# Some 25 entries of a fused four-layer kernel's order tables moved by one step or less

## The chip, the cores and the metric

The kernel runs on one core of one Trainium2 chip. The metric is device time in microseconds (us) of one launch; the figure for a kernel is the median of its runs. All engines of the core are in use: TensorE for matmuls (PE, and PEld for its weight loads), VectorE (DVE), ScalarE (ACT), GpSimd (POOL), and SyncE (SP), which here does nothing but issue DMAs.

## The reference

Four residual layers A, B, A, B on x of 2048 tokens by 512, fp32, 32 heads of 16. Layer A is linear attention with a learned feature map (per head a 16x16 product, then softmax of it and of its negative). Layer B cuts the sequence into four segments of 512 tokens; in each it does causal softmax attention and mixes it with a read of a memory that the segments before it have filled.

```python
# layer A
pq, pk = einsum(q, w_phi), einsum(k, w_phi)
phi = lambda t: concatenate([softmax(t), softmax(-t)])
kv, z = einsum("bhsf,bhsd->bhfd", phi(pk), v), phi(pk).sum over s
o = (phi(pq) @ kv) / (phi(pq) . z + 1e-6);  x = x + o @ wo
# layer B, for each of the four segments s
p = softmax(qs @ ks.T * scale + causal mask);  a_dot = p @ vs
a_mem = (elu1(qs) @ M) / (elu1(qs) . z + 1e-6)
o = g * a_mem + (1 - g) * a_dot
M, z = M + elu1(ks).T @ vs, z + elu1(ks).sum();  x = x + o @ wo
# both layers take layernorm(x) as input
```

## The kernel before

Matrix products of weight and activation are done as three products of a high and a low part (`hh`/`hl`, `oh`/`ol`, the two `w` tiles). The program is one long list: every engine takes its instructions in the order in which the Python code emits them (`Ordered` and `held` add a dependency from each instruction to the one before it on its engine). What is emitted when is set by tables of text. So an instruction that waits holds up everything behind it on its own engine.

Layer A has two passes. Pass 2 of a layer A runs into the layer B that follows: `A20` of its pieces are emitted before B's steps begin, and the rest is given out in the slots from step -9 to step 1 until `LEFT` units of TensorE work are spent.

Layer B is a loop over steps `k` from `BEGIN` = -25 to 163. One layer B has 32 pairs of head groups `m` (8 per segment), and each takes five steps, so a segment has 40 steps. A cell `5.1` of segment 2 is step 2 x 40 + 5 x 5 + 1 = 106. Cells of segment 0 stand in `FIRST`, of segments 1 and 2 in `GAPS`, of segment 3 in `LAST` (first layer B) or `FINAL` (second one), steps below 0 in `BEFORE`. In each step there is a fixed part, in this order:

1. `attend`: two to four products into the PSUM tile `lg`, of which there is one buffer; ACT takes exp of it in one instruction of 128x1024 (`P<-lg`), POOL masks diagonals. The next step's `lg` can't begin before this exp has ended.
2. `maxima`: products into the PSUM tiles `mx` and `my`, one buffer each, and DVE reductions of them (`junk` or `mx`/`my` out, `mxs` the result). The next step's `mx` product waits for these reductions.
3. `weighted` in some steps: the products `pv<-P,v`, 16 of them in a row.

Around that stand the table's entries, and things that are due at a half step after another event (`at`, `due`). The entries and events that the change and the prediction speak of:

- `out/2`: two quarters of an output projection of the segment before (three products `g<-w,oh`, `g<-w,oh`, `g<-w,ol` to a quarter); the last quarter ends with a DVE add `xr<-g,xr`. `x2` loads that `xr` row.
- `q2+/1`, `v/2`, `p/3`: quarters of a projection of the next segment, of the next layer's values, of the last output projection.
- `ln`: four transposes of a normalized tile of the next layer's input (`g<-ident,x`), an ACT copy (`hh<-g`) and a DVE subtraction (`hl<-g,hh`).
- `t1` (transposes of keys, copied by ACT), `m2` (update of the memory), `a3` (read of the memory: `pv<-tb,mem`, `g<-tb,mem`, then ACT copies `ot<-pv` and `mmq<-g`), `fin` (`g<-ident,U`, DVE division), `pt` (`end_turn`: transposes, `ot<-g,ot`, `oh<-ot`, `ol<-ot,oh`).
- `max` (`put_maxima`): a transpose `g<-ident,mxs`, an ACT copy `mt<-g`, and a DMA.
- `JOIN`: when a finished output block is scaled and added (POOL), copied to its high part by ACT (`oh<-tmp`, fourth number) and reduced to its low part by POOL (`ol<-tmp,oh`, fifth). Its three rows hold for segment 0, segments 1 and 2, and segment 3.
- `INVERT`: denominators gathered by a DMA (`dm<-den` or `dn<-den`), inverted by DVE (`RECIPROCAL`), stored and loaded again. `READ[2]` shifts this whole chain for the two blocks of segment 3 that get only their memory part so.
- `GATHER`: when the two DMAs from a finished `U` are issued. `n`, `N`, `w`, `load`, `pre`, `x1`: loads and parts of norms.

PSUM tile `g` has three buffers in turn. Trace and program name tiles without numbers: `P` is a `P4` tile, `ta` is `ta1`, `tb` is `tb2` or `tb3`, `e` is an `e8` tile, `w` is any weight tile. Nearly all instructions have the line of a helper, L180 (all but TensorE), L202 (matmul) or L206 (transpose).

## Time and profile before

| | |
|---|---|
| runs (3), device time | 1403.5, 1406.56 and 1407.33 us; median 1406.56 us |
| profiled execution, first to last instruction | 1401.3 us; no other time of this execution is given |
| TensorE matmul busy | 1369.1 us, 98% |
| VectorE, ScalarE, GpSimd busy | 963.9, 810.9, 734.1 us (69%, 58%, 52%) |
| granted TensorE clock | 1.000 |
| steps of the first layer B | from 292.4 us (step 0) to 714 us (step 159) |
| steps of the second layer B | from 979.0 us (step 0) |

Steps are told apart in the trace by their products into `lg`. The median is 5.3 us longer than the span; the three runs lie 2.2 to 6.0 us above it. Busy TensorE time takes in the tail of each matmul, so that a wait shorter than such a tail shows as no gap; where two rows of the timeline start farther apart than others of the same kind, that is such a wait.

### The profile page before, as it was taken

How to read it: one execution, taken by the hardware profiler on the slowest of the kernel's cores; microseconds unless marked ns; L12 is line 12 of the kernel's file. 1: busy time of each engine (PE TensorE's matmuls, PEld its weight loads, DVE VectorE, ACT ScalarE, POOL GpSimd, SP SyncE). 2: the span in 40 equal slices, each digit the busy share in tenths (PEclk: the TensorE clock that was granted, in tenths of full speed). 3: DMA queues.
4: the chain of work that ended last, by engine and by line, in shares of the span. 5: the costliest groups of instructions: out<-in, count | busy, mean ns of one | idle time of the engine just before them, and what ended most of it. 6: DMA issues, size and time to landing. Idle time of an engine off the chain costs nothing.

```text
span 1401.3 us, 33234 instructions
## 1 busy us (share of the span) xinstructions
PE 1369.1 (98%) x12070; PEld 943.2 (67%) x12070; DVE 963.9 (69%) x3030; ACT 810.9 (58%) x1244; POOL 734.1 (52%) x1073
## 2 busy tenths in 40 slices
PE   9999999999999999999999999999999999999998
PEld 7787778766666666655568887886655666666554
DVE  5766888677667657667647768958776666666674
ACT  5555445447686677566544434553566866765654
POOL 1677755324656656554534346642356565754643
PEclk9999999999999999999999999999999999999999
DMA  5369285645756656567631104855465566565552
GB/s 199 118 216 330 99 280 175 187 122 162 201 131 190 169 137 183 158 171 196 197 134 39 62 31 125 275 162 155 137 172 171 148 178 180 143 172 142 155 158 69
DMA packets 135730, 225.27 MB, mean 161 GB/s; under 512 B 21328, under 2 KB 39888, under 8 KB 135568
## 3 DMA queue, kind: packets, MB, share of 16 engines
q1 hardware_dynamic: 134464, 222.91, 54.2%
q8 instruction: 97, 1.59, 0.5%
q14 instruction: 65, 0.53, 0.1%
q10 hardware_dynamic: 1104, 0.24, 0.1%
HBM read 116.39 MB, written 43.25 MB: 114 GB/s over the span
## 4 chain that ended last, share of the span: by engine, by line
PE 78%; DVE 8%; ACT 5%; POOL 4%; issue 2%; DMA 2%; SPq 0%; DVEq 0%; ACTq 0%; POOLq 0%
PE g L202 47%; PE pv L202 9%; PE lg L202 9%; PE mx L202 4%; PE g L206 3%; PE my L202 3%; ACT P L180 2%; PE lg L206 1%; POOL P L180 1%; POOL tb L180 1%; DVE es L180 1%; POOL tmp L180 1%; DVE junk L180 1%; DVE my L180 1%; DVE mx L180 1%
## 5 line engine op out<-in xcount | busy, mean ns | idle before, releaser
L180 ACT ACTIVATE P<-lg 128x1024 f32<-128x1024 f32 x316 | 324.5, 1027 | 167.5 <-PE lg L202 159.6
L180 POOL TENSOR_SCALAR_AFFINE_SELECT P<-P 128x256 f32<-128x256 f32 (+1 forms) x448 | 190.3, 439 | 388.9 <-ACT P L180 388.1
L180 DVE CUSTOM_DVE_ANT_0 junk<-mx,mask 128x128 uint8<-128x128 f32 (+2 forms) x384 | 146.6, 420 | 101.8 <-PE my L202 72.7
L202 PE MATMUL g<-hh,wqk 128*128 128x512 f32 x512 | 186.3, 411 | 0.7 <-ACT mt L180 0.7
L202 PE MATMUL lg<-e,e 64*128 64x512 f32 (+1 forms) x1010 | 166.0, 386 | 6.4 <-ACT P L180 6.0
L180 DVE CUSTOM_DVE_ANT_0 mx<-mx,mask 128x512 f32<-128x512 f32 x128 | 89.2, 697 | 120.1 <-PE my L202 95.4
L202 PE MATMUL g<-w,oh 128*128 128x512 f32 x508 | 169.2, 414 | 0.5 <-ACT hh L180 0.4
L202 PE MATMUL pv<-P,v 128*32 128x512 f32 (+3 forms) x2048 | 165.5, 439 | 0.6 <-ACT ot L180 0.5
L202 PE MATMUL my<-e,e 63*128 63x256 f32 (+3 forms) x519 | 147.2, 343 | 4.2 <-DVE mxs L180 3.0
L202 PEld LDWEIGHTS lg<-e,e 64*128 64x128 f32 x1010 | 79.9, 184 | 102.9 <-issue 44.9
L202 PE MATMUL mx<-e,e 63*128 63x256 f32 (+3 forms) x519 | 145.9, 334 | 1.9 <-DVE mxs L180 1.6
L180 DVE CUSTOM_DVE_ANT_0 junk<-my,mask 128x128 uint8<-128x128 f32 (+2 forms) x384 | 146.8, 420 | 0.0
L202 PE MATMUL g<-w,hh 128*128 128x512 f32 x448 | 143.9, 402 | 0.3 <-ACT hh L180 0.3
L202 PEld LDWEIGHTS pv<-P,v 128*32 128x32 f32 x2048 | 53.5, 109 | 102.9 <-issue 95.3
L202 PEld LDWEIGHTS g<-hh,wqk 128*128 128x128 f32 x512 | 96.2, 188 | 33.7 <-issue 13.4
L202 PEld LDWEIGHTS g<-w,oh 128*128 128x128 f32 x508 | 87.6, 189 | 30.8 <-issue 13.4
L202 PE MATMUL g<-w,ol 128*128 128x512 f32 x254 | 100.8, 397 | 2.3 <-DVE ol L180 2.2
L180 DVE DVE_READ_ACCUMULATOR2_ANT mxs<- 128x1 f32 x1024 | 100.4, 98 | 0.0
L202 PE MATMUL g<-hl,wqk 128*128 128x512 f32 x256 | 100.3, 392 | 0.0
L202 PEld LDWEIGHTS mx<-e,e 63*128 63x128 f32 (+1 forms) x519 | 90.8, 185 | 10.0 <-DVE mxs L180 5.0
L202 PEld LDWEIGHTS g<-w,hh 128*128 128x128 f32 x448 | 80.3, 188 | 22.6 <-issue 6.0
L202 PEld LDWEIGHTS my<-e,e 63*128 63x128 f32 (+1 forms) x519 | 84.2, 185 | 15.7 <-DVE mxs L180 8.3
(190 smaller groups left out, 2848.2 us busy)
## 6 DMA issues: line engine op xcount, KB each, us to landing
e<-ta SPq DMA_DIRECT2D x384, 128.0 KB
wqk<-wqk SPq DMA_DIRECT2D x64, 512.0 KB
x<-x SPq DMA_DIRECT2D x48, 256.0 KB
xr<-x SPq DMA_DIRECT2D x32, 256.0 KB
x<-xr SPq DMA_DIRECT2D x28, 256.0 KB
tmp<-U SPq DMA_DIRECT2D x56, 128.0 KB
KN<-inv SPq DMA_DIRECT2D x28, 256.0 KB
pq<-tb SPq DMA_DIRECT2D x24, 256.0 KB
```

The source lines that it names most:

```text
L180: i = f(*a, **k)
L202: return held(nc.tensor.matmul(*a, **k))
L206: return held(nc.tensor.transpose(*a))
```

## The change

It moves entries of the tables. No instruction is added or removed: every engine issues the same instructions, in another order. The core of it, with unchanged cells left out:

```diff
-LEFT = 24900
+LEFT = 25500
-A20 = 103
+A20 = 102
-GATHER = (3.5, 1.5)
+GATHER = (3.5, 2.0)
-INVERT third row, block 0: (2.5, 4.5, 5.5, 7.5)
+INVERT third row, block 0: (2.5, 4.5, 6.0, 7.5)
-READ = (1.5, 2.5, 1, 12.5)
+READ = (1.5, 2.5, 2, 12.5)
-JOIN second row (9.5, 9.5, 11.5, 12, 13.5) for all four blocks
+JOIN second row (9.5, 9.5, 11.5, 13, 13.5), and block 3 (9.5, 9.5, 10.5, 13, 13.5)
 BEGINNING: one "k" ahead of "v1 c2"
 FIRST
-3.4 ... w | 4.0 w | 4.2 m2 | 4.3 k0+/1
+3.4 ... w w | 4.3 m2 k0+/1
-7.0 n | 7.1 max q2+/4~
+7.0 n q2+/1 | 7.1 max q2+/3~
 GAPS
-0.3 k2/1~ v3/2 | 1.4 t1 k3/2~
+0.3 k2/1 v3/2 | 1.3 k3/2 t1 | 1.4 k3/2~
-2.1 max out/3 | 2.3 ln ln
+2.1 max out/2 | 2.3 ln out/1 ln
-3.4 t2 ... | 4.2 m2 | 5.1 max out/3 | 5.4 t3 ...
+3.3 ... t2 | 4.3 ... m2 | 5.1 out/3 max | 5.3 ... t3 ...
 LAST
-6.1 max v/2 | 7.1 pt p/3 v/2
+6.1 v/2 | 6.2 max | 7.1 pt v/2 p/3
 FINAL
-3.0 x1 | 4.3 pre out/2 x2 | 4.4 a3 out/2 | 5.1 x3 out/2 max | 5.3 fin out/2 | 7.3 p/4 fin
+3.1 max x1 | 4.2 pre | 4.3 out/2 x2 | 4.4 a3 out/2 out/2 | 5.1 x3 max | 5.4 fin pre | 7.4 fin p/3
 BEFORE
-{-25: "q0 load", -23: "v0", -10: "v2 n", -4: "max q2~"}
+{-25: "v0 q0 load", -10: "n", -8: "v2", -4: "q2~", -3: "max"}; one "n" from -18 to -16
```

What that does to the order shows at three places.

ScalarE in the first layer B, segment 1, from cell 4.4 (step 64) to the exp of cell 5.1 (step 66), before the change:

```order
L180 ACTIVATE P_1163_6176<-lg_6175 128x1024
L180 CAST oh_6193<-tmp_5682 128x512
L180 ACTIVATE ot_6200<-pv_6196,bd 68x512
L180 ACTIVATE mmq_6201<-g_6197,bd 68x512
L180 CAST ta_1174_6221<-g_6206 128x512
L180 ACTIVATE P_1180_6235<-lg_6234 128x1024
L180 ACTIVATE tb_1176_6224<-g_6206 128x512
L180 ACTIVATE tb_1177_6225<-g_6206 128x512
L180 ACTIVATE P_1186_6265<-lg_6264 128x1024
```

The same stretch with the change:

```order
L180 ACTIVATE P_1163_6174<-lg_6173 128x1024
L180 ACTIVATE ot_6197<-pv_6193,bd 68x512
L180 ACTIVATE mmq_6198<-g_6194,bd 68x512
L180 CAST ta_1172_6218<-g_6203 128x512
L180 ACTIVATE P_1178_6232<-lg_6231 128x1024
L180 CAST oh_6243<-tmp_5682 128x512
L180 ACTIVATE tb_1174_6221<-g_6203 128x512
L180 ACTIVATE tb_1175_6222<-g_6203 128x512
L180 ACTIVATE P_1186_6265<-lg_6264 128x1024
```

The copy `oh<-tmp` has moved from ahead of the exp of step 65 to behind it; this happens eight times in each layer B, at steps 64, 74, and so on to 134.

TensorE in the first layer B, segment 2, cell 2.3 (step 93), before the change:

```order
L202 MATMUL lg_7272<-e_457_2902,e_458_2903 128x256 x2
L202 MATMUL lg_7272<-e_457_2902,e_458_2903 128x384 x2
L202 MATMUL mx_7281<-e_438_2819,e_437_2818 128x256
L202 MATMUL my_7282<-e_438_2819,e_437_2818 128x256
L202 MATMUL mx_7281<-e_438_2819,e_437_2818 128x384
L202 MATMUL my_7282<-e_438_2819,e_437_2818 128x384
L206 MATMUL g_7293<-ident,x_6088 128x128 x4
L206 MATMUL g_7300<-ident,x_6281 128x128 x4
L202 MATMUL lg_7310<-e_457_2902,e_458_2903 128x256 x4
```

The same step with the change:

```order
L202 MATMUL lg_7270<-e_457_2902,e_458_2903 128x256 x2
L202 MATMUL lg_7270<-e_457_2902,e_458_2903 128x384 x2
L202 MATMUL mx_7279<-e_438_2819,e_437_2818 128x256
L202 MATMUL my_7280<-e_438_2819,e_437_2818 128x256
L202 MATMUL mx_7279<-e_438_2819,e_437_2818 128x384
L202 MATMUL my_7280<-e_438_2819,e_437_2818 128x384
L206 MATMUL g_7291<-ident,x_6088 128x128 x4
L202 MATMUL g_7215<-w_4345,oh_6975 128x512
L202 MATMUL g_7215<-w_4346,oh_6975 128x512
L202 MATMUL g_7215<-w_4345,ol_6976 128x512
L206 MATMUL g_7301<-ident,x_6281 128x128 x4
L202 MATMUL lg_7308<-e_457_2902,e_458_2903 128x256 x4
```

One quarter of an output projection, which stood in cell 2.1, now stands between the two groups of transposes; so it is in segments 1 and 2 of both layers.

SyncE's DMAs in the first layer B, segment 3, cells 3.1 to 3.4 (steps 136 to 139), before the change:

```order
L180 DMA ot_8757<-mmq_8758 64x512
L180 DMA inv_8869<-dn_8765 128x128
L180 DMA dm_8871<-den_8795 128x64
L180 DMA tb_1768_8892<-x_13_99 128x512
L180 DMA x_8_110<-xr_8761 128x512
L180 DMA w_8820<-awv_188 128x512
L180 DMA w_8821<-awv_189 128x512
L180 DMA xr_8911<-x_9_95 128x512
L180 DMA w_8820<-awv_188 128x512
```

The same stretch with the change:

```order
L180 DMA ot_8754<-mmq_8755 64x512
L180 DMA inv_8888<-dn_8762 128x128
L180 DMA tb_1767_8890<-x_13_99 128x512
L180 DMA x_8_110<-xr_8758 128x512
L180 DMA w_8820<-awv_188 128x512
L180 DMA w_8821<-awv_189 128x512
L180 DMA xr_8909<-x_9_95 128x512
L180 DMA dm_8911<-den_8795 128x64
L180 DMA w_8820<-awv_188 128x512
```

The gather `dm<-den` has moved behind five other DMAs; on VectorE the `RECIPROCAL` that reads it has moved from ahead of the two maxima of step 140 to behind them.

## Prediction

> **What bounds the kernel now.** I read the page first, then TensorE's waits, then the timeline around each wait that the change touches, step by step.

> ```profile
> span 1401.3 us, 33234 instructions
> PE 1369.1 (98%) x12070; PEld 943.2 (67%) x12070; DVE 963.9 (69%) x3030; ACT 810.9 (58%) x1244; POOL 734.1 (52%) x1073
> ```

> TensorE is busy for all but 32.2 us of the span. The change removes no product, so all that it can win is waiting: those 32 us, and the waits too short to show as a gap. TensorE's waits, longest totals (us, times, longest):

> ```profile
> PE lg L202 <- ACT P L180: 6.0, 16, 0.9
> PE my L202 <- DVE mxs L180: 3.0, 13, 0.3
> ```

> The reader is to see two kinds. Either the exp of one step ends late, and the next step's `lg` product, which has one buffer, waits for it; or the maxima of one step end late on VectorE, and the next `mx` and `my` products wait. Both happen in a step that holds little TensorE work behind one whose ScalarE or VectorE work is late. Moving 0.6 us of TensorE work into the short step, or the late work out of the way, is what can help; in a step that TensorE fills by itself a move is worth nothing.

> **The change part by part.** I take each wait that stands beside a moved entry, and ask what is left of it.

> *Copy `oh<-tmp` (JOIN).* ScalarE and TensorE in the first layer B, segment 1:

> ```profile
> 443.75 0.51 PE L202 MATMUL lg<-e,e 64*128 64x512 f32 x2
> 445.64 0.50 PE L202 MATMUL lg<-e,e 64*128 64x512 f32 x2
> ...
> 457.63 0.62 ACT L180 CAST oh<-tmp 128x512 fp32r<-128x512 f32 x1 [1.99 <-POOL tmp L180]
> 458.55 0.50 PE L202 MATMUL lg<-e,e 64*128 64x512 f32 x2
> 459.77 1.03 ACT L180 ACTIVATE P<-lg 128x1024 f32<-128x1024 f32 x1
> 460.69 1.08 ACT L180 ACTIVATE tb<-g 128x512 f32<-128x512 f32 x2
> 460.86 0.50 PE L202 MATMUL lg<-e,e 64*128 64x512 f32 x2 [0.36 <-ACT P L180]
> 463.98 0.30 PEld L202 LDWEIGHTS lg<-e,e 64*128 64x128 f32 x4 [0.37 <-issue]
> ...
> 1311.56 0.50 PE L202 MATMUL lg<-e,e 64*128 64x512 f32 x2 [0.38 <-ACT P L180]
> ```

> The copy waited 1.99 us for GpSimd's join, and the copies behind it pushed the exp of step 65 to 459.77, although its `lg` products began at 458.55. Step 65 took 2.31 us (458.55 to 460.86); step 60, of the same make, took 1.89 (443.75 to 445.64). So 0.42 us was lost, of which 0.36 shows as a gap. With the copy behind the exp, this exp starts when `lg` is done. Eight of the sixteen waits of `lg` for ScalarE follow a moved copy: at 460.86 the first, at 1311.56 the last, with gaps of 0.36, 0.29, 0.32, 0.11 in the first layer B and 0.36, 0.29, 0.34, 0.38 in the second, 2.45 us together. Times 0.42/0.36 that is 2.9 us, which I take. At the other eight copies nothing waits now. Ends: below 0 (a rival, below), and 6.7 if all sixteen copies cost 0.42.

> What is queued behind the copy in its new place: two copies `tb<-g` (1.08 us) and the exp of step 66. If exp 65 starts 0.6 us earlier, at 459.2, exp 66 can start at 459.2 + 1.0 + 0.6 + 1.1 = 461.9 and ends at 462.9; step 67's `lg`, now at 463.98, would want to go at 463.6. 0.7 us are to spare, and GpSimd's `ol<-tmp,oh` behind the copy isn't read before the next out quarter.

> *One out quarter from 2.1 to 2.3 in segments 1 and 2.* First layer B, segment 2, steps 94 to 96:

> ```profile
> 537.14 0.28 PE L202 MATMUL mx<-e,e 63*128 63x256 f32 x1
> 537.26 1.28 DVE L180 TENSOR_TENSOR hl<-g,hh 128x512 fp32r<-128x512 f32 x2
> 537.49 0.35 PE L202 MATMUL my<-e,e 63*128 63x256 f32 x1
> 537.72 0.59 PE L202 MATMUL pv<-tb,mem 64*68 64x512 f32 x1
> 538.00 0.64 PE L202 MATMUL g<-tb,mem 64*68 64x512 f32 x1
> ...
> 541.06 0.69 DVE L180 TENSOR_TENSOR hl<-g,hh 128x512 fp32r<-128x512 f32 x1 [1.15 <-ACT hh L180]
> 542.00 0.50 PE L202 MATMUL lg<-e,e 64*128 64x512 f32 x2 [0.32 <-ACT P L180]
> 543.12 0.38 PE L202 MATMUL my<-e,e 63*128 63x256 f32 x1 [0.27 <-DVE mxs L180]
> ```

> `my` started 0.35 us after its `mx`, with which it pairs elsewhere, because VectorE's maxima were late; `g<-tb,mem` started 0.28 after its `pv`, because the two `hl<-g,hh` had not yet freed a buffer of `g`. The two are 0.63 us. With the quarter between the two transposes the first `hl` is done before the second is needed. At four places (segments 1 and 2, two layers) that is 2.5 us; I take 2.0, since VectorE must still do both subtractions. Ends: 0, where VectorE stays the later one, and 2.5. Step 91, which loses the quarter, keeps two and a `max`; VectorE's slack in it is the cover, and without it the wait comes back at step 92 with at most the same 0.63 us a place.

> In step 95 VectorE waited for ScalarE's third `hh` (idle 1.15 before 541.06), which stood behind `oh<-tmp`; so `my` was 0.27 late at 543.12. The moved copy frees this too: 0.3 us in all, of 0 to 0.5 for two layers.

> *A quarter of q2 from 7.1 to 7.0, and `max` from step -4 to -3.*

> ```profile
> 381.16 0.31 PE L202 MATMUL mx<-e,e 63*128 63x256 f32 x1
> 381.74 0.38 PE L202 MATMUL my<-e,e 63*128 63x256 f32 x1 [0.27 <-DVE mxs L180]
> ...
> 279.78 0.28 PE L206 MATMUL g<-ident,mxs 128*16 128x128 f32 x1 [0.50 <-DVE xr L180]
> 280.41 0.50 PE L202 MATMUL g<-hh,wqk 128*128 128x512 f32 x1 [0.35 <-ACT mt L180]
> ```

> Step 36 began before VectorE had finished step 35: `my` is 0.58 us behind its `mx`, 0.27 of it a gap. The quarter, three products, gives step 35 more than that. 0.4 a layer, 0.8 us; ends 0 and 1.2. Before step 0, the transpose of the maxima waited 0.50 us for a buffer and q2 another 0.35 for the copy behind it. With q2 first, the 0.50 stays, now before q2, and the 0.35 goes: 0.7 us in two layers, ends 0 and 1.7.

> *The memory part's denominators (READ) in the first layer B, segment 3.*

> ```profile
> 655.53 0.51 SPq L180 DMA_DIRECT2D dm<-den  x1
> 658.74 0.32 SPq L180 DMA_DIRECT2D xr<-x  x1
> 659.87 0.55 DVE L180 RECIPROCAL dm<-dm 128x64 f32<-128x64 f32 x1 [1.54 <-DMA dm<-den]
> 661.13 0.38 PE L202 MATMUL mx<-e,e 63*128 63x256 f32 x1 [1.21 <-DVE mxs L180]
> 661.78 0.38 PE L202 MATMUL my<-e,e 63*128 63x256 f32 x1 [0.27 <-DVE mxs L180]
> ...
> 665.25 0.57 PE L202 MATMUL lg<-e,e 64*128 64x256 f32 x4
> ...
> 677.16 0.32 SPq L180 DMA_DIRECT2D dn<-den  x1
> 679.40 0.95 DVE L180 RECIPROCAL dn<-dn 128x128 f32<-128x128 f32 x1 [0.38 <-DMA dn<-den]
> ```

> `RECIPROCAL dm` waited 1.54 us for its DMA with the maxima of step 140 queued behind it, and TensorE waited 1.21 + 0.27 us in step 141. After the change two maxima go ahead of it, and those of step 141 are behind it. Its DMA goes out behind five others, near 659.1 (658.74 plus that row's 0.32). Between issue and use lay 4.34 us here and 2.24 us at 677.16, so it lands between 661.3 and 663.4. Step 141 has two out quarters and two value quarters behind its `mx` product, and ends near 665.25 - 1.48 = 663.8 (665.25 is where step 142 began, 1.48 the two waits). VectorE needs 0.55 us for the reciprocal and 1.4 for the maxima behind it (from 659.87 + 0.55 to the `my` product of 661.78): done at 663.2 at best, at 665.3 at worst, against 664.2, 0.4 into step 142, where its `my` product would start. So between 1.5 and 0.4 us are won; I take 0.9. [...]

> *LAST 7.1: values ahead of the output products.*

> ```profile
> 703.78 0.30 PEld L202 LDWEIGHTS g<-w,oh 128*128 128x128 f32 x2 [0.54 <-ACT oh L180]
> ```

> The weight loads of the first products after `pt` waited 0.54 us for `oh`. Two value quarters now stand in between and cover it: 0.5 us, ends 0 and 1.0.

> *FINAL: two quarters from 5.1 to 4.4, `fin` from 5.3 to 5.4.* Second layer B, steps 145, 146 and 150:

> ```profile
> 1356.03 1.29 PE L202 MATMUL pv<-P,v 128*32 128x512 f32 x16 [0.52 <-ACT ot L180]
> 1357.02 0.69 DVE L180 TENSOR_TENSOR xr<-g,xr 128x512 f32<-128x512 f32 x1 [3.12 <-issue]
> 1357.52 0.51 PE L202 MATMUL lg<-e,e 64*128 64x512 f32 x2 [0.20 <-ACT P L180]
> 1358.43 0.38 PE L202 MATMUL mx<-e,e 63*128 63x256 f32 x1 [0.40 <-DVE mxs L180]
> 1359.08 0.38 PE L202 MATMUL my<-e,e 63*128 63x256 f32 x1 [0.27 <-DVE mxs L180]
> ...
> 1367.75 0.49 PE L202 MATMUL lg<-e,e 64*128 64x512 f32 x2 [0.94 <-ACT P L180]
> ```

> Four gaps, 0.52 + 0.20 + 0.40 + 0.27 = 1.39 us. In step 144 the two quarters give ScalarE time for the copy `ot` and VectorE time for the row that the add `xr<-g,xr` waited for (3.12 us idle). The add is as late as before; TensorE comes to it 1.4 us later. I take 1.1, ends 0 and 1.4. At 1367.75 the exp of a short step ends last (0.94); `fin` puts four transposes, 0.6 us, into that step: 0.6, ends 0 and 0.9.

> *At nothing:* `t1`, `t2`, `t3` and `m2` one step on (their steps are filled by TensorE, and no wait of it stands at them), `GATHER` (no other DMA lies between its old and new place), `w`, `n`, `x1`, `pre`, `v0`, `LEFT`, `A20` and the `k` of BEGINNING: their DMAs and pieces go one step earlier or later, with several steps until they are used. If that cover is gone, each would show as a gap of some tenths; I allow for that in the next line.

> *Sum:* 2.9 + 2.0 + 0.3 + 0.8 + 0.7 + 0.9 + 0.5 + 1.1 + 0.6 = 9.8 us. Against it 1.8 us of waits that form anew: 0.3 at the out quarters of cell 3.1, where `ol` now comes later, and the rest at steps that lose work (2.1, 5.1 and 5.3 of FINAL). It is an estimate, a fifth of the sum. Net 8.0: a span of 1393.3 us. The median lies 5.3 us above the profiled span, and I keep that: 1398.6 us.

> **The rivals.** *The waits form anew one step on.* For it: in most steps `lg`, `mx` and `my` have one buffer each, so TensorE that is let go early meets the next exp or maxima; every 1.9 us step ends close behind its exp. Against it: the steps x.1 are 3.1 us long. If half of the first three terms (2.6) and all of READ and of steps 144 to 146 (2.0) come back, 9.8 - 1.8 - 4.6 = 3.4 us are left: 1403.2 us.

> *Everything goes.* With each term at its upper end (without the eight copies at which nothing waits: 3.4) and no new wait, 3.4 + 2.5 + 0.5 + 1.2 + 1.7 + 1.5 + 1.0 + 1.4 + 0.9 = 14.1 us: 1392.5 us. For it: most of the waits are of the same few kinds, and the places repeat in both layers.

> *Slower.* One mechanism: the moved copy itself waits for GpSimd's join, as at 457.63 (1.99 us), now between two exps. Then the exp of each step x.1 is late. It decides from 0.7 us of waiting on, the slack found above. At sixteen places with 0.6 us each, 9.6 us are lost, against 9.8 - 2.9 - 0.3 - 1.8 = 4.8 won elsewhere: 1411.4 us. Against it: the copy is a step later, so that the join has 2 us more; only eight waits show at all.

> That the change does nothing, because the order is kept by something else, is excluded: the orders of all engines differ.

> **How the numbers follow.** The forecast, from 1395 to 1402, has 0.57; everything goes 0.17; the waits form anew 0.18; slower 0.08. A difference under 0.3% (4.2 us) is about what a measurement of this kernel can't tell from none. The forecast and the second case lie beyond it: faster 0.74. The third lies within: 0.18. Slower 0.08. The range leaves out about 0.1 at either end: from a little below the second case, 1391, to above the third by the 2 us that the runs of one kernel lie apart about their median, 1405.5.

> **What would show it.** Right: step 65 takes 1.9 us and the list of waits has under 3.5 us of `lg` for ScalarE (6.0 now); `my` for VectorE's maxima under 2 us; no gap over 0.5 us at step 141 of the first layer B; TensorE's busy time about as now and its idle time near 24 us. Wrong: gaps at the steps x.2 (exp of x.1 late behind the copy), a longer wait of `RECIPROCAL dm` with a gap at step 142, or waits of `g<-w,ol` for GpSimd at cell 3.1. The prediction fails if steps that now show no gap lose some tenths each in the segments' forty steps: 0.1 us in 40 of 320 steps would take half of the gain.

## The result, and the profile after

| | before | after |
|---|---|---|
| median device time, first chip (6 runs each) | 1405.66 us (1401.72 to 1407.33) | 1392.86 us (1391.25 to 1395.59) |
| ratio, with its 95% interval | | 0.9917 (0.9900 to 0.9933) |
| ratio on a second chip (23 and 6 runs) | | 0.9934 (0.9922 to 0.9946) |
| span of the profiled execution | 1401.3 us | 1393.9 us |
| TensorE busy, and the rest of the span | 1369.1, 32.2 us | 1367.5, 26.4 us |

The change makes the kernel 0.7 to 0.8% faster: 9 to 13 us, where 8.0 were forecast. 1392.86 us lies in the range (1391 to 1405.5), 5.7 us under the number, and next to the rival "everything goes" (1392.5), though not for its reason. The page after the change (each engine's own count is as before; the 15 instructions more in the first line are semaphore waits):

```profile
span 1393.9 us, 33249 instructions
PE 1367.5 (98%) x12070; PEld 944.8 (68%) x12070; DVE 963.2 (69%) x3030; ACT 813.4 (58%) x1244; POOL 735.6 (53%) x1073
```

TensorE's waits (us, times, longest):

```profile
PE lg L202 <- ACT P L180: 4.7, 11, 0.7
PE my L202 <- DVE mxs L180: 2.2, 9, 0.3
PE mx L202 <- DVE mxs L180: 1.3, 1, 1.3
```

The two kinds of wait have fallen from 6.0 to 4.7 and from 3.0 to 2.2 us (3.4 and 2.1 us in a second trace). One of 1.3 us, `mx` waiting for maxima, has stayed; it is at step 142 now, where the gather `dm<-den` was to be cured.

*The moved copy.* ScalarE and TensorE in the first layer B, segment 1, steps 65 to 67, after the change:

```profile
456.11 0.50 PE L202 MATMUL lg<-e,e 64*128 64x512 f32 x2
456.70 1.03 ACT L180 ACTIVATE P<-lg 128x1024 f32<-128x1024 f32 x1
457.61 0.62 ACT L180 CAST oh<-tmp 128x512 fp32r<-128x512 f32 x1
457.99 0.50 PE L202 MATMUL lg<-e,e 64*128 64x512 f32 x2
461.24 0.56 PE L202 MATMUL lg<-e,e 64*128 64x256 f32 x4
```

The exp of step 65 now starts 0.59 us behind `lg`, not 1.22, and the copy stands behind it without a wait. Step 65 takes 1.88 us (2.31 before), as the prediction named for this part, and `lg` of step 67 (461.24) has no wait. Step 66 is 0.12 us longer than before (3.25).

*The moved gather.* SyncE, VectorE and TensorE, first layer B, steps 141 and 142, after the change:

```profile
655.58 0.32 SPq L180 DMA_DIRECT2D dm<-den  x1
...
659.59 0.55 DVE L180 RECIPROCAL dm<-dm 128x64 f32<-128x64 f32 x1 [3.46 <-DMA dm<-den]
660.92 0.46 PE L202 MATMUL mx<-e,e 63*128 63x512 f32 x1 [1.26 <-DVE mxs L180]
661.61 0.47 PE L202 MATMUL my<-e,e 63*128 63x512 f32 x1 [0.23 <-DVE mxs L180]
```

VectorE waits 3.46 us for the gather and TensorE 1.26 + 0.23 us, as much as before (1.21 + 0.27), one step later. Then this, the same core's busy times, granted clock and DMA share (the last three columns: clock, DMA, GB/s) in four stretches:

```profile
659.00:662.00 3.00, 1.51 (x7) 0.66 (x6) 2.41 (x10) 1.02 (x1) 0.00 (x0) 1.00 0.96 250
662.00:664.00 2.00, 2.00 (x21) 0.82 (x22) 1.42 (x5) 0.28 (x1) 0.00 (x0) 0.70 1.00 214
664.00:666.00 2.00, 2.00 (x11) 1.48 (x10) 0.93 (x7) 1.43 (x2) 1.86 (x3) 0.50 0.85 238
666.00:670.00 4.00, 4.00 (x23) 2.51 (x22) 1.95 (x12) 1.02 (x1) 2.60 (x5) 0.98 0.69 218
```

Behind the wait TensorE ran at half its clock for 3.4 us. The first trace of before shows nothing of the kind, and so this trace lost 1.6 us here (steps 141 to 143 take 12.47 us, 10.90 before).

### The profile page after: what moved, and what is told of

Read it like the earlier page. It is cut to its first block, busy times and chain, and to the rows that moved or that the text cites. A ratio compares the mean times of both kernels' runs of the same rounds, so it can differ in the third digit from the quotient of the medians.

```text
span 1393.9 us, 33249 instructions
## 1 busy us (share of the span) xinstructions
PE 1367.5 (98%) x12070; PEld 944.8 (68%) x12070; DVE 963.2 (69%) x3030; ACT 813.4 (58%) x1244; POOL 735.6 (53%) x1073
## 3 DMA queue, kind: packets, MB, share of 16 engines
q8 instruction: 97, 1.59, 0.5%
## 4 chain that ended last, share of the span: by engine, by line
PE 83%; DVE 7%; DMA 3%; ACT 3%; POOL 1%; issue 1%; SPq 0%; ACTq 0%; DVEq 0%; POOLq 0%
PE g L202 49%; PE pv L202 11%; PE lg L202 9%; PE mx L202 5%; PE g L206 3%; PE my L202 3%; PE lg L206 2%; ACT P L180 1%; DVE es L180 1%; POOL P L180 1%; DVE junk L180 1%; DMA w<-bwo 1%; PE pv L206 1%; SPq L180 0%; ACT hh L180 0%
## 5 line engine op out<-in xcount | busy, mean ns | idle before, releaser
L180 ACT ACTIVATE P<-lg 128x1024 f32<-128x1024 f32 x316 | 324.5, 1027 | 144.1 <-PE lg L202 135.6
L180 POOL TENSOR_SCALAR_AFFINE_SELECT P<-P 128x256 f32<-128x256 f32 (+1 forms) x448 | 191.1, 442 | 378.7 <-ACT P L180 376.3
L180 DVE CUSTOM_DVE_ANT_0 junk<-mx,mask 128x128 uint8<-128x128 f32 (+2 forms) x384 | 146.5, 419 | 103.0 <-PE my L202 74.9
L202 PE MATMUL g<-hh,wqk 128*128 128x512 f32 x512 | 186.8, 412 | 1.7 <-DVE xr L180 1.4
L202 PE MATMUL lg<-e,e 64*128 64x512 f32 (+1 forms) x1010 | 166.3, 387 | 4.9 <-ACT P L180 4.7
L202 PE MATMUL g<-w,oh 128*128 128x512 f32 x508 | 169.6, 415 | 0.4 <-ACT hh L180 0.4
L180 DVE CUSTOM_DVE_ANT_0 mx<-mx,mask 128x512 f32<-128x512 f32 x128 | 89.3, 697 | 115.9 <-PE my L202 93.6
L202 PE MATMUL pv<-P,v 128*32 128x512 f32 (+3 forms) x2048 | 165.9, 439 | 0.0
L202 PE MATMUL my<-e,e 63*128 63x256 f32 (+3 forms) x519 | 147.6, 344 | 2.7 <-DVE mxs L180 2.2
L202 PEld LDWEIGHTS lg<-e,e 64*128 64x128 f32 x1010 | 80.1, 184 | 101.0 <-issue 44.0
L180 DVE CUSTOM_DVE_ANT_0 junk<-my,mask 128x128 uint8<-128x128 f32 (+2 forms) x384 | 146.8, 420 | 0.0
L202 PE MATMUL g<-w,hh 128*128 128x512 f32 x448 | 144.4, 403 | 0.2 <-ACT hh L180 0.2
L202 PE MATMUL mx<-e,e 63*128 63x256 f32 (+3 forms) x519 | 142.1, 331 | 1.3 <-DVE mxs L180 1.3
L202 PEld LDWEIGHTS pv<-P,v 128*32 128x32 f32 x2048 | 53.4, 109 | 102.0 <-issue 92.6
L202 PEld LDWEIGHTS g<-hh,wqk 128*128 128x128 f32 x512 | 96.2, 188 | 36.0 <-issue 10.9
L202 PEld LDWEIGHTS g<-w,oh 128*128 128x128 f32 x508 | 87.9, 189 | 29.3 <-issue 13.5
L202 PE MATMUL g<-w,ol 128*128 128x512 f32 x254 | 100.9, 397 | 1.9 <-DVE ol L180 1.9
L180 DVE DVE_READ_ACCUMULATOR2_ANT mxs<- 128x1 f32 x1024 | 100.4, 98 | 0.0
L202 PE MATMUL g<-hl,wqk 128*128 128x512 f32 x256 | 100.3, 392 | 0.0
L202 PEld LDWEIGHTS mx<-e,e 63*128 63x128 f32 (+1 forms) x519 | 90.9, 186 | 8.8 <-issue 4.8
L202 PEld LDWEIGHTS g<-w,hh 128*128 128x128 f32 x448 | 80.0, 188 | 23.0 <-issue 6.3
L180 DVE CUSTOM_DVE_ANT_0 my<-my,mask 128x512 f32<-128x512 f32 x128 | 93.7, 732 | 0.0
```

The lines of the kernel that those rows point to most:

```text
L180: i = f(*a, **k)
L202: return held(nc.tensor.matmul(*a, **k))
```

## The experiments

A step's length is the distance between the first `lg` products of two steps. It repeats within 0.1 us from trace to trace of one kernel at nearly all steps, so differences of some tenths can be read from single traces; the device time of a kernel scatters by about 2 us about its median, single runs by up to 5.7. Each edit below was made to the kernel before unless it says otherwise.

**Both kernels a second time**, without an edit.

> The kernel before, unchanged, for a second trace of it. Theory one (the two profiled executions tell the change): span 1400 to 1404 us, and the steps of its two layers B, which are 421.5 us (first, step 0 to 159) and 406.5 us (second) in the first trace, come out within 0.3 us of that; TensorE's step 0 of the first layer B starts at 292 +- 0.5. Rival (executions differ by stretches, so that one trace against one says little under 2 us): the start of step 0 moves by 1 us or more, as it did from 292.4 before to 289.8 with the change, or one layer differs by over 1 us.

> The changed kernel again, for a second trace and a tight time. Theory one: the halved clock that its first trace shows for some 4 us from 662.4 on (granted 0.50, behind the 1.26 us wait of step 142 of the first layer B) is a thing of single executions; then the stretch of steps 141 to 143, 12.5 us in the first trace and 10.9 before, is 10.9 to 11.2 here with the same wait of about 1.3 us, and the span is 1389.5 to 1391.5. Rival: the wait makes the drop each time; then the stretch is 12.4 or more again. Time against the kernel before: 0.990 to 0.993.

Before: 1405.03 us (one run), span 1403.3. Outside one place its layers B repeat the first trace; step 141 takes 7.61 us, not 5.83. This trace has the halved clock too, behind a wait of 1.49 + 0.26 us. After: 1394.43 us, span 1393.8, the clock halved again behind 1.38 + 0.23 us: the rivals of both expectations held, but through this one place. The first trace of before was without a drop that the second has, and that four of the eight traces with READ as before have (last section). Compared in the same condition, 1403.28 - 1393.79 = 9.5 us of span: the step 0 of the first layer B comes 3.05 us earlier, the first layer B's steps are 2.22 shorter, the stretch between the layers 1.45, the second layer B's steps 3.37, and the rest 0.60 longer.

**The copy alone (JOIN).**

```diff
-((9.5, 9.5, 11.5, 12, 13.5),) * 4
+((9.5, 9.5, 11.5, 13, 13.5),) * 4
```

> The kernel before with the copy oh<-tmp moved behind the exp of step x.0 (fourth number of JOIN's second row, 12 to 13), and nothing else. Theory one (the copy delays the exp, and this exp delays TensorE): the gaps of lg for ScalarE at steps 66, 86, 96 and 126 go, step 65 takes 1.9 us instead of 2.31, and the eight places give 2.4 to 2.9 us: ratio 0.998. Rival one (waits form anew): step 65 takes 1.9 us but step 66 or 67 the 0.4 us more, and the layers take as long as before: ratio 1.000. Rival two: the copy now waits between two exps for GpSimd's join, and lg waits at steps x.2: ratio 1.002 or more.

Ratio 0.9991 (0.9980 to 1.0001), which alone can't tell theory one from none. The steps can: 65, 75, 85, 95 and 135 are 0.43, 0.12, 0.30, 0.39 and 0.34 us shorter in the first layer, 65, 75, 85, 95 and 125 0.43, 0.13, 0.28, 0.41 and 0.37 in the second, 3.2 us together. Step 67 is 0.12 us longer in both layers (its `pv<-P,v` start later behind `lg`; why isn't shown), so 3.0 us are left. All eight gaps of `lg` behind a moved copy are gone, and no moved copy waits for GpSimd's join, where three in each layer did (1.99, 1.41 and 0.26 us in the first). Theory one, a little above its size; rival one shows in those 0.12 us alone, rival two nowhere. Unexpected, step 146 of the second layer fell from 3.73 to 2.50 us: the add `xr<-g,xr`, which stood idle 3.12 us in before, came in time here. Why its row was there in time isn't shown; four kernels whose edits don't touch this step (the quarter, LEFT and A20, BEFORE, all ahead of step 0) have it 0.17 to 0.43 us shorter too, so the 1.2 us can't be put down to JOIN alone.

**One quarter alone (GAPS, cells 2.1 and 2.3).**

```diff
-2.1 max out/3 | 2.2 m1 | 2.3 ln ln |
+2.1 max out/2 | 2.2 m1 | 2.3 ln out/1 ln |
```

> The kernel before with one quarter of the output projection moved from cell 2.1 to between the two ln of cell 2.3 in segments 1 and 2 (four places), and nothing else. Theory one (a quarter lets VectorE finish the first hl<-g,hh before a buffer of g is needed): steps 51 to 54 and 91 to 94 together take 0.6 us less each, 2.5 us in the two layers: ratio 0.998; steps 54 and 94 lose 0.68, step 51 and 91 lose 0.69, steps 53 and 93 win 0.70. Rival (VectorE has as much to do as before and stays the later one): steps 51 to 54 take as long in sum: ratio 1.000.

Ratio 0.9996 (0.9985 to 1.0007). Steps 51, 53 and 54 do what was expected (-0.69, +0.69, -0.69 us), step 56 gives 0.19 back: 0.50 us a layer. In segment 2 the same -0.69, +0.69, -0.68 is undone by +0.19 in step 92 and +0.49 in step 95: nothing is left. ScalarE and TensorE in step 95 of this kernel:

```profile
538.69 0.62 ACT L180 CAST oh<-tmp 128x512 fp32r<-128x512 f32 x1 [0.18 <-POOL tmp L180]
539.01 0.50 PE L202 MATMUL lg<-e,e 64*128 64x512 f32 x2
540.37 0.57 ACT L180 CAST hh<-g 128x512 fp32r<-128x512 f32 x1
540.83 1.03 ACT L180 ACTIVATE P<-lg 128x1024 f32<-128x1024 f32 x1
541.92 0.50 PE L202 MATMUL lg<-e,e 64*128 64x512 f32 x2 [0.47 <-ACT P L180]
```

`lg` of step 95 came earlier, but the exp behind it did not: `oh<-tmp`, two copies and `hh` stand ahead of it. So the next `lg` waits 0.47 us. It is the queue that JOIN shortens; with both in the changed kernel steps 90 to 100 are 0.61 us shorter, with JOIN alone 0.49. The quarter is worth 0.5 and 0.1 us a layer there, 1.2 in all.

**What lies ahead of step 0.**

```diff
-LEFT = 24900, A20 = 103
+LEFT = 25500, A20 = 102
-BEFORE: -23: "v0" | -18: "n", -17: "v1 n", -16: "n" | -10: "v2 n", -4: "max q2~"
+BEFORE: -25: "v0 ..." | -17: "v1 n", -16: "n n" | -10: "n", -8: "v2", -4: "q2~", -3: "max"
 BEGINNING: one k ahead of "v1 c2"
```

> The kernel before with the entries that lie ahead of step 0 alone: LEFT, A20, BEFORE and the k of BEGINNING. My prediction had 0.7 us for max and q2 in BEFORE and nothing for the rest. Theory one (the rest counts too): step 0 of the first layer B starts at 289.6 to 290.2 us instead of 292.4 to 292.9 (three traces of kernels without these entries), the stretch from the end of the first layer B's steps to the second's step 0 is 263.4 to 264 instead of 265.1, and the ratio is 0.997 to 0.998; the waits of mx and my near 270 and 273 us are gone. Rival (only the two entries count and the rest of the difference is scatter of the first layer A, whose start of step 0 was 291.1 in one trace): step 0 at 291.6 to 292.2, 264.6 between the layers, ratio 0.999 to 1.

Ratio 0.9978 (0.9967 to 0.9988), step 0 at 289.12 us, 263.43 between the layers: theory one. TensorE around the pairs of `mx` and `my` ahead of step 0, with a product that all kernels have (`g<-w,oh`, waiting for `hh`) at the left end and step 0 at the right; first before:

```profile
239.25 0.70 PE L202 MATMUL g<-w,oh 128*128 128x512 f32 x2 [0.19 <-ACT hh L180]
...
265.89 0.38 PE L202 MATMUL mx<-e,e 63*128 63x256 f32 x1
266.36 0.38 PE L202 MATMUL my<-e,e 63*128 63x256 f32 x1
...
269.57 0.39 PE L202 MATMUL mx<-e,e 63*128 63x256 f32 x1
270.14 0.35 PE L202 MATMUL my<-e,e 63*128 63x256 f32 x1 [0.18 <-DVE mxs L180]
...
272.86 0.50 PE L202 MATMUL mx<-e,e 63*128 63x512 f32 x1
273.55 0.50 PE L202 MATMUL my<-e,e 63*128 63x512 f32 x1 [0.19 <-DVE mxs L180]
...
292.44 0.50 PE L202 MATMUL lg<-e,e 64*128 64x512 f32 x2
```

The same with these entries moved:

```profile
237.51 0.71 PE L202 MATMUL g<-w,oh 128*128 128x512 f32 x2 [0.18 <-ACT hh L180]
...
266.87 0.38 PE L202 MATMUL mx<-e,e 63*128 63x256 f32 x1
266.87 0.38 PE L202 MATMUL my<-e,e 63*128 63x256 f32 x1
...
269.57 0.49 PE L202 MATMUL mx<-e,e 63*128 63x512 f32 x1
270.15 0.49 PE L202 MATMUL my<-e,e 63*128 63x512 f32 x1
...
289.12 0.50 PE L202 MATMUL lg<-e,e 64*128 64x512 f32 x2
```

From the first row to the last it is 53.19 us before and 51.61 now, with the same 353 products between. This distance depends little on what the executions do earlier: 53.2 in five traces of kernels without these entries (53.3 in the second layer), 51.6 in six of the seven with them (51.6 in the second). So 1.6 to 1.7 us a layer are theirs. In before, `my` starts 0.47, 0.57 and 0.69 us behind its `mx`, of which only 0.09, 0.18 and 0.19 are gaps; with the entries moved one such distance of 0.58 is left. That is about 1.1 of the 1.6 us. The waits at `max` and q2, 0.50 and 0.35 us in before, are one of 0.67.

Two parts of it alone, first LEFT and A20, then the row BEFORE:

> The kernel before with LEFT and A20 alone, one look. The entries ahead of step 0 together moved step 0 of the first layer B from about 292.1 to 289.4 us and shortened the stretch between the layers by 1.8. Theory one (LEFT hands out more products of layer A in the slots from step -9 on, in which TensorE waited for maxima): the waits near 270, 273 and 273.7 (0.18, 0.13, 0.19) go here already, and the stretch between the layers is 263.8 to 264.6. Rival (it is the entries of BEFORE: the other slots for v0, v2, n, max and q2): these three waits stand as before, and the stretch is 265.0 to 265.6.

> The kernel before with the row BEFORE alone (v2 from step -10 to -8, v0 from -23 to -25, n one step, max from -4 to -3). LEFT and A20 alone left the waits near 266, 273 and 274 and the start of step 0 as before (293.2 us, 265.9 between the layers). Theory one (v2 in step -8 stands between two pairs of mx and my, so that VectorE's maxima are done when TensorE comes to the next pair): the gaps of my and mx near 270 and 273 go, step 0 of the first layer B starts at 289 to 290 us, the stretch between the layers is 263.4 to 264.4, ratio 0.996 to 0.998. Rival (it takes both, the slots and LEFT's units, since more units stand between): at most half of it, step 0 at 290.5 to 292, 264.5 to 265.5 between the layers, ratio 0.998 to 1.

| | ahead of step 0, first layer | second layer | between the layers |
|---|---|---|---|
| before | 53.2 us | 53.3 us | 265.1 us |
| LEFT and A20 | 53.5 | 53.5 | 265.9 |
| BEFORE | 52.4 | 52.7 | 264.3 |
| all | 51.6 | 51.6 | 263.4 |

LEFT and A20 alone win nothing and still have three such waits (0.27, 0.26 and 0.20 us), so its rival held. BEFORE alone (ratio 0.9984, 0.9973 to 0.9994) wins about half of what all win. That is what its rival said, and the ratio is in its range; but 264.3 us between the layers is in theory one's, and of the two gaps that theory one named the one near 270 is gone and the one near 273 (0.19) is not. The start of step 0 (293.0 us) fits neither, since layer A ahead of it was slow in this trace. The parts do not add: +0.3 and -0.8 make -1.6 together.

How much the `k` of BEGINNING does, ahead of the first row, is not settled: that row stands between 237.86 and 240.59 us in seven traces without it, between 237.02 and 238.05 in seven with it, and it was not run alone.

**The table FINAL alone.**

> The kernel before with the table FINAL of the change, one look. Moving the copy oh<-tmp alone shortened step 146 of the second layer from 3.73 to 2.50 us. Theory one (the same wait, two cures, so that the two do not add): FINAL alone shortens steps 144 to 148 by 1.0 to 1.4 us in sum, and step 150's gap of 0.94 for ScalarE falls to 0.35; steps 120 to 157 of the second layer take 87.6 to 88.2 us, against 89.5 before. Rival (FINAL adds nothing at steps 144 to 148, all of it is the copy's): their sum stays within 0.3 us of before's 14.4.

One run, 1403.88 us. Steps 144 to 148 change by +1.39, -0.86, -1.90, +1.06 and -0.34, 0.65 us less together; steps 150 to 157 take 0.32 less, and what follows 0.43 more. That is 0.5 us in all, between theory one and the rival, and little more than the 0.17 to 0.43 us by which step 146 is shorter in kernels that leave this table alone: how much is FINAL's is not settled. The gap at step 150 fell from 0.94 to 0.36 as expected. Steps 140 to 150 of the second layer are 1.44 us shorter in the changed kernel, 1.25 with JOIN alone.

**The gather mended.** Made to the changed kernel; the reciprocal stays one step later, its gather goes back:

```diff
-READ = (1.5, 2.5, 2, 12.5)
+READ = (1.5, 2.5, 1, 12.5)
-self.invert(s, c, k + READ[2], range(1, 2), INVERT[2][c])
+self.invert(s, c, k + READ[2], range(1, 2), (2.5, 5.5, 6.0, 7.5))
```

> The changed kernel with its gather dm<-den back at the place of before (READ 1), while the reciprocal that reads it stays where the change put it, one step later. Theory one (the gather needs some 4 us whatever stands in front of it, so moving both by two steps only moved the wait, and a wait of 1.25 us or more makes the clock halve behind it): the gaps of 1.26 to 1.38 and 0.23 at step 142 go, no stretch shows a granted clock of 0.5 near there, steps 140 to 150 of the first layer B take 28.5 to 29 us instead of 31.9, the span is 1390 to 1391, and the time is 0.2% under the changed kernel's: ratio to before 0.990 to 0.9915. Rival (the DMA is late here too, or the wait turns up at the next reader, inv<-dm): 30 us or more in these steps and a ratio of 0.992 to 0.994 as the changed kernel.

```profile
650.21 0.58 SPq L180 DMA_DIRECT2D dm<-den  x1
655.23 0.54 DVE L180 RECIPROCAL dm<-dm 128x64 f32<-128x64 f32 x1
655.35 0.58 SPq L180 DMA_DIRECT2D KN<-inv  x1
662.84 1.28 POOL L180 TENSOR_TENSOR tmp<-tmp,KN 128x512 f32<-128x512 f32 x1 [5.83 <-DMA e<-ta]
668.67 0.68 ACT L180 ACTIVATE ot<-pv,bd 68x512 f32<-68x512 f32 x1 [3.67 <-POOL tmp L180]
669.40 1.07 PE L202 MATMUL pv<-P,v 128*32 128x512 f32 x8 [1.53 <-ACT ot L180]
```

The reciprocal at 655.23 waits for nothing. Steps 141 to 143 take 8.81 us (12.47 and 12.58 in the changed kernel), and the clock is full. It was full in the first trace of before too, where they take 10.90: a wait that shows as gaps of 1.48 us costs 2.09. But steps 140 to 150 take 29.91 us, not 28.5 to 29: GpSimd's `tmp<-tmp,KN`, whose rows `KN<-inv` were issued at 655.35, begins only at 662.84 (the trace puts the wait down to `e<-ta`, a transfer issued behind these rows; in the next three traces of kernels with this gather it names `mmq<-inv`, issued with them, or `KN<-inv`); ScalarE's copy `ot` waits for GpSimd's join, and TensorE for the copy, 1.53 us in step 145. The first layer B is 2.4 us shorter than in the changed kernel's second trace; the time is 1394.70 us, ratio 0.9937 (0.9923 to 0.9950), no better. In this trace 1.3 us of it were lost again in the second layer A and at steps 146 and 147 of the second layer B. So theory one held at its place and failed on the time, where the rival's range held.

**And `m2` back** (the same kernel, `m2` again in the cells 4.2 of FIRST and GAPS).

> The same as the run before it, and m2 back in cell x.2 in segments 0 to 2 of both layers (six places). Theory one (step x.2 cannot get shorter than about 1.9 us, its exp with what stands around it, so that of the 0.5 us of m2 only 0.3 were won there and 0.5 paid in x.3): steps 62 and 63, 102 and 103 take 0.17 to 0.2 us less together at each of four places, steps 22 to 24 0.3 and 0.5 less in the two layers: 1.5 us, ratio to before 0.989 to 0.990. Rival (the steps after them got shorter in exchange): the sums of steps 20 to 30, 60 to 70 and 100 to 110 stay within 0.15 us of the changed kernel's 23.9, 28.5 and 28.5.

> The kernel with gather and m2 back, again, beside the one above on the same chip. Theory one (the removed wait and clock drop are worth more than the scatter of the two layers A): ratio to before 0.9905 to 0.992 as in its first timing (0.9917, 0.9904 to 0.9931), steps 140 to 150 of the first layer B between 28.7 and 29.9 us, no granted clock of 0.5 before the last 5 us of the span. Rival (its first timing, of four runs, was lucky): 0.993 to 0.994, as the changed kernel.

First timing 1392.77 us, ratio 0.9917 (0.9904 to 0.9931); second 1391.83 us, 0.9914 (0.9900 to 0.9927). Steps 62 and 63, 102 and 103 are 0.17 to 0.20 us shorter together at each of the four places, 0.75 in all, as expected; at steps 22 to 24 0.1 is lost in the first layer and 0.14 won in the second, so there theory one failed, and with it its ratio (0.989 to 0.990). Of what was expected of the second timing the ratio came, but steps 140 to 150 took 30.09 us (28.73 in the first trace), and the clock dropped once. With `m2` gone, step 62 falls only from 2.24 to 1.94 us, while step 63 grows by 0.47 to 0.50. Both timings lie under the 0.9934 of the second chip, and the first chip gave 0.9917 for the changed kernel: that this version is faster than the changed kernel is not shown. The second trace has a halved clock of its own, in the first layer's steps 14 and 15, behind three short waits:

```profile
322.86 0.56 PE L202 MATMUL lg<-e,e 64*128 64x256 f32 x4 [0.44 <-ACT P L180]
323.97 0.38 PE L202 MATMUL my<-e,e 63*128 63x256 f32 x1 [0.27 <-DVE mem L180]
326.06 0.48 PE L202 MATMUL my<-e,e 63*128 63x256 f32 x1 [0.33 <-DVE mxs L180]
```

And the four microseconds behind them, busy times, clock (0.57), DMA share and GB/s as above:

```profile
326.00:330.00 4.00, 3.94 (x19) 2.65 (x23) 2.29 (x10) 2.38 (x4) 2.94 (x3) 0.57 0.24 53
```

**And those rows a step earlier** (in the third row of INVERT, block 0: 5.5 and 6.5 for 6.0 and 7.5).

> The kernel of the run before (gather back, m2 back) and the loads KN<-inv and mmq<-inv of the block 0 of segment 3 a step earlier, ahead of two weight loads (6.5 for 7.5, the store ahead of it 5.5 for 6). Theory one (in step 145 of the first layer B, ScalarE's ot<-pv waits for GpSimd's join, which waits for these rows; that is the wait behind the one that the mended gather took away, 1.53 us in one trace and 0.16 in the other): GpSimd's tmp<-tmp,KN starts 1 us or more earlier, the gap at step 145 is 0 and the one of 0.68 at step 146 smaller; steps 140 to 150 take 28.2 to 28.6 us against 29.9 and 28.7. Ratio to before 0.989 to 0.991. Rival (the DMA queues are full here, and the rows come no earlier, or the weights behind them come late): steps 140 to 150 take 28.7 to 30 us again, ratio 0.991 to 0.993.

```profile
654.33 0.58 SPq L180 DMA_DIRECT2D KN<-inv  x1
659.49 1.29 POOL L180 TENSOR_TENSOR tmp<-tmp,KN 128x512 f32<-128x512 f32 x1 [3.66 <-DMA KN<-inv]
...
672.59 0.46 PE L202 MATMUL mx<-e,e 63*128 63x512 f32 x1 [0.38 <-DVE mxs L180]
673.27 0.46 PE L202 MATMUL my<-e,e 63*128 63x512 f32 x1 [0.23 <-DVE mxs L180]
```

GpSimd begins 6.13 us behind the start of step 141 (6.93 and 7.64 without this edit) and the gap at step 145 is gone, but step 147 now waits 0.38 + 0.23 us for maxima and is 1.1 and 0.4 us longer than in those two traces. Its maxima stand behind the add `xr<-g,xr`, which waits 2.87 us for its row. Steps 140 to 150: 29.53 us, beside 28.73 and 30.09 of the kernel without this edit; ratio 0.9926 (0.9913 to 0.9938). The rival's ranges held, though the rows did come earlier: a third late thing stood behind the second.

## Why the prediction was right or wrong

*The bound.* Right in kind: the gain came from waits of TensorE, of `lg` for exp and of `my` for maxima above all. But the busy time did not stay. Between the two traces with the same drop, before again and after again, it falls from 1371.6 to 1367.2 us and the rest of the span from 31.7 to 26.6: of the 9.5 us, 4.4 had been counted as busy. The list of what would show it was too hopeful: `lg` for ScalarE 4.7 and 3.4 us in the two traces after (under 3.5 said), `my` 2.2 and 2.1 (under 2), idle 26.4 and 26.6 (near 24). No gap stands at step 141, but a longer wait of `RECIPROCAL dm` with a gap at step 142 does, which was on the list of what would be wrong.

*Term by term:*

| term | forecast, us | measured, us |
|---|---|---|
| copy (JOIN) | 2.9, and 0.3 freed in step 95 | 3.2 at the steps x.0, 0.2 lost at step 67; step 146 of the second layer 1.2 shorter, not settled |
| out quarter | 2.0 | 1.0 alone, 1.2 beside JOIN |
| quarter of q2 from 7.1 to 7.0 | 0.8 | 0.9 (steps 35 and 36 of the changed kernel: +0.89 and -1.35 or -1.37; not run alone) |
| `max` and q2 in BEFORE, other entries ahead of step 0 | 0.7, nothing | 3.3 together |
| READ | 0.9 | 0; the wait only moved |
| LAST 7.1 | 0.5 | 0.35 (steps 155 and 156 of the changed kernel: +0.28 and -0.63; not run alone) |
| FINAL | 1.7 | 0.5 at most alone; beside JOIN 0.2 at steps 140 to 150, then 0.3 won and 0.6 lost: nothing in sum |
| `m2` | 0 | 0.75 lost |

Two pieces of the change belong to no term. Step 86 is 0.3 us shorter in each layer of the changed kernel, and not with JOIN or the quarter alone. And 1.4 of the 9.5 us lie ahead of the row that stands 53.2 us ahead of step 0, where the traces of the kernels overlap.

*The step that failed most* is the line "At nothing", and with it the term for BEFORE. I priced LEFT and A20 at nothing, which holds for them alone but not beside BEFORE (52.4 us ahead of step 0 without them, 51.6 with them), and left out that `v2` moves by two steps (as `v0` does; the title's "one step or less" doesn't hold for these two), although the trace shows three waits of `mx` and `my` near 270 and 273 us. The rule that a late product costs more than its gap, which I used for `my` at steps 36 and 94, gives 0.47 + 0.57 + 0.69 us a layer here, of which about 1.1 were won.

*READ.* Two steps failed: the middle between two landing times, and the end of step 141. I let the gather land 2.24 to 4.34 us behind an issue near 659.1; it went out 0.24 us behind the start of step 141, where I had it 0.3 ahead, and its reader began 4.01 us later, the late end. The row with 2.24 us, at 677.16, had three transfers of 256 KB just ahead, issued 2.2 to 3.2 us before it; the moved gather had five. What sets the time from issue to landing is not shown. In place of the 0.4 us that the late end was to win, nothing was won, since step 141 ended 3.76 us after its start and not 4.4: I had taken off its two gaps (1.48 us), where the wait cost 2.09. That the wait would be seen at `my` of step 142 was nearly right: it is at that step's `mx`. This is a wait that forms anew one step on, as that rival said, at one of its three places.

*The quarter.* "Ends: 0, where VectorE stays the later one": in segment 2 it was ScalarE that stayed late, which I had not named for this term.

*New waits* were estimated at 1.8 us. What is traced to an entry is 0.75 us of `m2`, whose short step x.2 gave up 0.30 us where step x.3 took 0.47 to 0.50, 0.24 at step 67 with JOIN alone, and 0.4 of FINAL behind step 157. A part of the rest is in steps 13, 14 and 22 to 24: `lg` of step 23 waits 0.55 and 0.74 us for the exp of step 22, which it does not in before. No run shows the entry that does it.

*From the span to the median.* I kept 5.3 us between them. That step is wrong: an execution's time is 1.7 us above its own span (1395.59 and 1393.9). Of the other 3.6 us, 1.8 may be what the second trace of before takes longer in step 141, 1.5 of it the halved clock, which the first one happened to be without; whether the median run had it is not shown, and the rest is not traced. The trace-to-trace 7.4 us so agree with the net 8.0 by chance: two traces with the same drop differ by 9.5. That the median landed in the range is partly luck too: terms that were too large (READ, the quarter, FINAL) stood beside one that was missing, ahead of step 0.

*The rival "slower"*, a copy waiting between two exps, shows nowhere: with JOIN alone, no moved copy waits for GpSimd's join.

## What to carry to other kernels

Price a wait by how far the two rows that belong together stand apart, not by the gap alone, and look at each such place before an entry near it is priced at nothing. When a late transfer is the cause, move the transfer and its reader apart; moving both moved the wait here. A cured wait can meet the next late thing a few steps on, so effects of entries near each other need not add: here JOIN and the quarter, BEFORE and LEFT.

## What the runs showed of the hardware that was not expected

| kernel | waits, us | idle in the stretch, us | steps 141 to 143, us | clock of 0.5 |
|---|---|---|---|---|
| BEFORE alone | 0.74 + 0.27 | 0.74 | 10.44 | no |
| copy alone | 1.00 + 0.26 | 0.73 | 10.70 | no |
| before | 1.21 + 0.27 | 1.13 | 10.90 | no |
| LEFT and A20 | 1.32 + 0.27 | 1.41 | 11.02 | no |
| after | 1.26 + 0.23 | 1.49 | 12.47 | yes |
| after again | 1.38 + 0.23 | 1.61 | 12.58 | yes |
| before again | 1.49 + 0.26 | 1.76 | 12.68 | yes |
| FINAL alone | 1.64 + 0.27 | 1.53 | 12.90 | yes |
| quarter alone | 1.77 + 0.27 | 1.96 | 12.95 | yes |
| all ahead of step 0 | 1.86 + 0.27 | 1.70 | 13.12 | yes |

The length less the waits is 9.42 to 9.44 us without the drop and 10.91 to 10.99 with it: 1.5 us, whatever the wait was. In the four traces of kernels with the gather mended the wait is gone and so is the drop at this place. Here are the stretch with the wait and the one behind it in two traces of this table, before again and then LEFT and A20:

```profile
659.16:662.57 3.41, 1.65 (x18) 0.79 (x10) 2.21 (x6) 1.20 (x2) 1.17 (x4) 1.00 1.01 357
662.57:665.98 3.41, 3.41 (x11) 2.49 (x9) 1.65 (x9) 0.27 (x1) 0.00 (x0) 0.50 0.96 292
```

```profile
658.97:662.38 3.41, 2.01 (x19) 0.69 (x19) 1.74 (x7) 1.82 (x2) 1.00 (x4) 1.00 0.93 297
662.38:665.79 3.41, 3.23 (x16) 2.48 (x16) 2.13 (x11) 0.27 (x1) 0.17 (x2) 1.00 0.94 274
```

The length of the wait alone does not decide: 1.49 us in all had a drop and 1.59 had none, nor had the 1.53 us at step 145 of the mended kernel. The end of a stretch cut these two, with 1.41 and 1.23 us idle ahead of it. So in this table a stretch with 1.49 us idle or more is followed by a drop, and one with 1.41 or less is not. Two stretches elsewhere don't fit: one with 0.74 us idle had a drop (the three waits of 0.44, 0.27 and 0.33 us in 3.2 us, shown above), and one with 1.78 near the end of the span of the copy alone had none. What else counts is open. The stretches begin at other places in each execution: the first rise came 4.91 us behind the first instruction in the first trace of before, and 7.43 us in the first trace after the change. Ahead of these drops TensorE was never idle for more than 1.86 us without a break.
